# Sums over 64 columns as pairs and fours of array columns, and a row tile's norm moved on VectorE, in a four-layer attention and MLP kernel

## The chip, the cores and the metric

The kernel runs on one core of a Trainium2 chip. The metric is the device time of one execution in microseconds, the median of three runs: 762.07 us before the change (761.74 to 762.75). A core has TensorE (called PE in the profile, with PEld for its weight loads), VectorE (DVE), ScalarE (ACT), GpSimd (POOL), and SyncE (SP), on whose queue this kernel issues its transfers.

## The reference

Four layers follow each other on a sequence of 2048 rows of 576 numbers: attention, MLP, attention, MLP, each behind a layer norm and with a residual. Both attention layers use the same weights, as do both MLP layers. Cut to what matters:

```python
def _A_ref(x, wqkv, wo):
    B, S, D = x.shape
    H = 32; Dh = D // H
    qkv = (x @ wqkv).reshape(B, S, 3, H, Dh).transpose(2, 0, 3, 1, 4)
    q, k, v = qkv[0], qkv[1], qkv[2]
    phi = lambda t: jnp.where(t > 0, t + 1, jnp.exp(t)) + 1e-6
    pq, pk = phi(q), phi(k)
    kv = jnp.einsum("bhsd,bhse->bhde", pk, v)
    z = jnp.einsum("bhsd->bhd", pk)
    num = jnp.einsum("bhqd,bhde->bhqe", pq, kv)
    den = jnp.einsum("bhqd,bhd->bhq", pq, z)[..., None] + 1e-6
    o = num / den
    return o.transpose(0, 2, 1, 3).reshape(B, S, D) @ wo

def _B_ref(x, w1, b1, w2, b2):
    y = _layernorm(x, axis=-1)
    h = _gelu(jnp.einsum("bsd,df->bsf", y, w1) + b1)
    return jnp.einsum("bsf,fd->bsd", h, w2) + b2

for _ in range(2):
    x = x + _A_ref(_layernorm(x, axis=-1), A_wqkv, A_wo)
    x = x + _B_ref(_layernorm(x, axis=-1), B_w1, B_b1, B_w2, B_b2)
```

The attention has no softmax: the sums `kv` and `z` over all rows are made first, and then every query row is multiplied by them.

## The kernel before

**Tiles.** The 2048 rows are 16 row tiles of 128 (`NT`). The 576 columns are four chunks of 128 and a last one of 64. Column halves of 288 (`HALF`) fit one PSUM bank. `yT` holds the normalized rows turned, for the products that contract over columns; `row_of` holds them as they are. The last 64 columns of each row tile lie in `v_ring`, 65 columns to a row tile: 64 of them are data and the 65th is ones (`tail_of(t)` in the second attention layer, which is layer 3 of the four, and `first_tail(t)` in the first).

**An attention layer.** `kv` is not made from `v`. Instead the layer makes K2 = rows-transposed times phi(keys), a matrix of 576 by 576, and multiplies it by the value weights afterwards (`kv_groups`). The column of ones beside the last 64 columns gives `z`, the sum of phi(keys), as row 65 of the last chunk. K2 is made in two column halves, since the accumulators of one half fill the PSUM banks that are to be had:

- *First pass*, one row tile after the other: `k_half(t, 0)` and `k_half(t, 1)` make both halves of the keys (L645), phi is taken on ScalarE and VectorE, one piece of the queries follows (`q_proj`, L614), and `rows_by_keys(t, 0)` adds the row tile to the first half of K2: one matmul for the last 64 columns and the ones (chunk 4, into `k2_tail`, 65 rows) and four for the others.
- *Second pass*: all 16 row tiles' chunk 4 first (L865 and L866: sixteen matmuls of 128 rows by 65 array columns, 288 moving columns), then the four other chunks, two row tiles' worth at a time (`sums`), with other work set between them. `z_stage` (L723 to L731) turns the row of sums into a column, by five matmuls with one column of the identity, and spreads it over the heads on VectorE (`zsel`). `den_stage` (L736) makes the denominators, forty matmuls of 32 array columns and 128 moving ones, whose outputs lie on four groups of 32 PSUM partitions. After them come the logarithm and exponential on ScalarE that make the reciprocal, the spreading of it, `kv_groups`, `kv_wo_half` and the output rows (`wo_stage`).

**Evacuations around the change.** The first half's `k2_tail` goes to `k2[4]`, rows 0 to 64, by one ScalarE copy (L673), ahead of the copies of the other chunks (L686). The second half's goes by one more. `k2[4]` has 128 rows; rows 64 to 127 are zeroed by GpSimd at the layer's start (L635). The value weights' last chunk in `wqkv_sb` likewise has 64 real rows and 64 zeroed ones (L217).

**Row tiles between layers.** While an MLP layer ends, each finished row tile is normalized for the next attention layer in steps (`LNPipe.tick`): statistics (L392, L393), the power -0.5 on GpSimd (L428), the norm into one of three tiles `y_ring` (L465), a store of the rows, and a turn of 32 by 32 blocks on VectorE (L297). Four turned row tiles are stored to DRAM together (L305) and loaded into `yT` (L320, L323). The last row tile (15) is finished when the attention layer has begun, so its statistics are ordered behind a phi on VectorE (`after="phi"`, L1088), while its norm and turn have no such order. `y_ring` is free during the second pass; in the first attention layer its tiles hold some early exponentials (`exp_tile`).

**Order.** TensorE's order is that of the program text (`pe`, L165). The other engines' orders come from a scheduler that keeps data dependencies and manual ones without a signal (`NOSYNC`). SP issues transfers in the order of its queue; at the start they are chained (`chained`, L157), the `x` rows and the attention weights ahead of the MLP weights.

**PSUM.** `ps_h` has four banks with one tag. A matmul into a bank waits for the engine that reads the bank's last content; two more tiles of two banks (`accA`, `accB`) hold the other chunks' sums.

Of the kernel before, what the change touches and what calls it, by code (L numbers as in the profile page):

```python
# [7 lines left out]
ACT = mybir.ActivationFunctionType  # L8
# [26 lines left out]
def build(tc, A_x, A_wqkv, A_wo, B_w1, B_b1, B_w2, B_b2, out, dbg=None, n_layers=4):  # L35
    nc = tc.nc
    dbg = dbg or {}
    with ExitStack() as ctx:
# [167 lines left out]
        for t in range(6, NT):  # L206
            load_x0(t)
        load_wqkv(2)
        nc.vector.memset(y_ring[NY - 1][:], 0.0)
        warm_ps = ps_h.tile([P, 512], F32, name="warm_ps", tag="h")  # L210

# [2 lines left out]
                pe(nc.tensor.matmul(warm_ps[:], lhsT=y_ring[NY - 1][:, 0:P], rhs=y_ring[NY - 1][:, 0:512],  # L214
                                    start=True, stop=True))

        nc.vector.memset(wqkv_sb[64:P, 4, :], 0.0)  # L217
        for vr in v_ring:
            nc.gpsimd.memset(vr[:], 0.0)
            nc.gpsimd.memset(vr[:].rearrange("p g c -> p (g c)")[:, 0:520].rearrange("p (t e) -> p t e", e=65)[:, :, 64:65], 1.0)  # L220
# [73 lines left out]
        def turn_rows(y, t, kind):  # L294

            c, j = divmod(t, TPC)
            turn = nc.vector.transpose(out=turned[:, :, j, :], in_=y[:, 0:D])  # L297
            if dve_last["sum"] is not None:
                tc.add_manual_dep(turn.ins, dve_last["sum"], NOSYNC, reason="rows are turned behind the sums")
            if j < TPC - 1:  # L300
                return
            home = y_d[state["turns"] % 2]
            state["turns"] += 1
            for i in range(4):
                store = nc.sync.dma_start(out=home[:, :, i * P:(i + 1) * P].rearrange("j r n -> r j n"),  # L305
                                          in_=turned[32 * i:32 * (i + 1), :, :, :].rearrange("r j t c -> r j (t c)"))
            landing.append([3, home, c, kind])
            if kind == "A" and c == NCB - 1:
                sp_last["turned"] = store.ins.name
# [32 lines left out]
        class LNPipe:  # L342
# [11 lines left out]
            def tick(self, transposes=1):  # L354
                land()
                for it in list(self.items):
# [77 lines left out]
                    elif st in (2, 3) and it["kind"] == "A" and it["evac"] == "act":  # L434
                        xt, t = it["xt"], it["t"]
                        tail = first_tail(t)[:, 0:64]
                        if it["norm"] == "pool":
                            for out, cols in ((xt[:, 0:4 * P], slice(0, 4 * P)), (tail, slice(4 * P, D))):
                                norm = nc.gpsimd.tensor_scalar(out=out, in0=xt[:, cols], scalar1=it["rstd"][:, 0:1],
                                                               scalar2=it["nmr"][:, 0:1], op0=ALU.mult, op1=ALU.add)  # L440
                            pool_last["norm"] = norm.ins.name
                        else:
                            for name, out, cols in ((f"n{t}", xt[:, 0:4 * P], slice(0, 4 * P)), (f"nt{t}", tail, slice(4 * P, D))):
                                norm = named(name, nc.vector.tensor_scalar(
                                    out=out, in0=xt[:, cols], scalar1=it["mv"][:, 0:1], scalar2=it["rstd"][:, 0:1],
                                    op0=ALU.subtract, op1=ALU.mult))
                            dve_last["norm"] = norm.ins.name
                        row_of[t] = xt
                        it["stage"] = 4
                        continue  # L450
                    elif st in (2, 3):
                        if sum(other["stage"] == 4 for other in self.items) == NY:
                            continue
                        y = y_ring[state["ycnt"] % NY]
                        state["ycnt"] += 1
                        xt = it["xt"]
                        if it["norm"] == "act":
                            nc.scalar.activation(out=y[:, 0:D], in_=xt[:, 0:D], func=ACT.Identity,
                                                 scale=it["rstd"][:, 0:1], bias=it["nmr"][:, 0:1])
                        elif it["norm"] == "pool":  # L460
                            norm = nc.gpsimd.tensor_scalar(out=y[:, 0:D], in0=xt[:, 0:D], scalar1=it["rstd"][:, 0:1],
                                                           scalar2=it["nmr"][:, 0:1], op0=ALU.mult, op1=ALU.add)
                            pool_last["norm"] = norm.ins.name
                        else:
                            norm = nc.vector.tensor_scalar(out=y[:, 0:D], in0=xt[:, 0:D], scalar1=it["mv"][:, 0:1],  # L465
                                                           scalar2=it["rstd"][:, 0:1], op0=ALU.subtract, op1=ALU.mult)
                            dve_last["norm"] = norm.ins.name
                        if it["kind"] == "B" and it["evac"] != "dma":
                            nc.gpsimd.tensor_copy(out=y[:, D:DPAD], in_=y[:, 4 * P:D])
                        if it["kind"] == "A" and it["evac"] == "dma":  # L470
                            c, j = divmod(it["t"], TPC)
                            nc.sync.dma_start(out=yrow_d[c, :, j], in_=y[:, 0:D])
                        it["y"] = y
                        it["stage"] = 4
                        continue
                    elif st == 4:
                        t = it["t"]
                        first_layer = it["kind"] == "A" and it["evac"] == "act"
                        y = it["xt"] if first_layer else it["y"]
                        if it["evac"] == "dma":  # L480
                            turn_rows(y, t, it["kind"])
                            self.items.remove(it)
                            continue
                        tp = ps_h.tile([P, 512], F32, name="tp", tag="h")
                        tp = tp[:, 0:DPAD // 2].bitcast(BF16).rearrange("p (k n) -> p k n", k=KD)
                        first = first_layer and t < 2
                        tp2 = tp
                        if first:
                            tp2 = ps_h.tile([P, 512], F32, name="tp2", tag="h")
                            tp2 = tp2[:, 0:DPAD // 2].bitcast(BF16).rearrange("p (k n) -> p k n", k=KD)  # L490
                        for k in range(KD):
                            block = first_tail(t, P) if first_layer and k == 4 else y[:, k * P:(k + 1) * P]
                            pe(nc.tensor.transpose(out=(tp if k < 3 else tp2)[:, k, :], in_=block, identity=ident[:]))  # L493
                        if first:
                            named(f"ca{t}", nc.scalar.copy(out=yT[:, 0:3, t * P:(t + 1) * P], in_=tp[:, 0:3, :]))
                            named(f"cd{t}", nc.vector.tensor_copy(out=yT[:, 3:KD, t * P:(t + 1) * P], in_=tp2[:, 3:KD, :]))
                        elif it["evac"] == "act":
                            turned_tile = nc.scalar.copy(out=yT[:, :, t * P:(t + 1) * P], in_=tp)
                            act_last["turned"] = turned_tile.ins.name
                            if first_layer and t < 5:  # L500
                                named(f"ca{t}", turned_tile)
                            elif act_last["exp"] is not None:
                                tc.add_manual_dep(turned_tile.ins, act_last["exp"], NOSYNC, reason="keys go on first")
                        else:
                            nc.vector.tensor_copy(out=yT[:, :, t * P:(t + 1) * P], in_=tp)
                        self.items.remove(it)
                        continue
# [100 lines left out]
        def layer_A(li, next_kind, pre_a1=None):  # L608
# [23 lines left out]
            kvwo = {}  # L632
            self_k = dict(pk={}, acc=None, rows={})
            k2 = [blk.tile([P, D], BF16, name="k2", tag="blk") for _ in range(KD)]
            nc.gpsimd.memset(k2[4][64:P, :], 0.0)  # L635
            first_pq = None
            if li == 0:
                first_pq = blk.tile([P, D], BF16, name="pq", tag="blk")
# [21 lines left out]
            def rows_by_keys(t, half, chunks=(4, 0, 1, 2, 3), done=True):  # L660
# [9 lines left out]
                    pe(nc.tensor.matmul(dst, lhsT=lhsT, rhs=pk, start=(t == 0), stop=(t == NT - 1)))  # L670
                cols = slice(half * HALF, (half + 1) * HALF)
                if 4 in chunks and t == NT - 1:
                    nc.scalar.copy(out=k2[4][0:65, cols], in_=self_k["tail"][0:65, 0:HALF])  # L673
                if not done:
                    return
                if t % 2:
# [7 lines left out]
                for i, copy in enumerate((nc.scalar.copy, nc.vector.tensor_copy)):  # L684
                    for j in range(2):
                        copy(out=k2[2 * i + j][:, cols], in_=self_k["acc"][i][:, j, 0:HALF])  # L686

            def kv_groups(groups):

# [33 lines left out]
            def z_stage():  # L723
                zp = ps_h.tile([P, 512], F32, name="z_ps", tag="h")
                for g in range(G):
                    pe(nc.tensor.matmul(zp[0:GR[g], g:g + 1], lhsT=k2[4][:, GO[g]:GO[g] + GR[g]], rhs=ident[:, 64:65],
                                        start=True, stop=True))
                nc.vector.tensor_tensor(out=zsel[0:126, 0:4, :], in0=head_sel[0:126, 0:4, :],
                                        in1=zp[0:126, 0:4].unsqueeze(2).to_broadcast([126, 4, H]), op=ALU.mult)
# [132 lines left out]
                rows_by_keys(NT - 1, 0)  # L862


            for t in range(NT):  # L865
                rows_by_keys(t, 1, (4,), done=False)  # L866
            left = list(range(NT))

            def sums(n):
# [316 lines left out]
```

## Time and profile before

| what | value |
|---|---|
| median of three runs | 762.07 us (761.74 to 762.75) |
| the profiled execution's own time | 762.17 us |
| its span in the trace | 760.5 us |
| instructions in the trace | 15743 |
| TensorE clock granted in the span | 1.0 |
| first attention layer's second-pass tail begins | 59.27 us |
| second attention layer's first key matmul begins | 383.93 us |
| second attention layer's second-pass tail begins | 431.54 us |

The span is counted from the first to the last instruction; the execution's time has 1.7 us more around it. In the timelines a row gives the start, the time from the first start to the last end, the engine, the line, the operation, and output and inputs, with "xN" where N alike follow each other. In brackets stands how long the engine was idle before and what ended that. A matmul's end is modelled and matmuls overlap: where they follow each other, the distance of their starts tells what one costs, not its length.

### The profile page before, as it was taken

Reading aid. Unit: us, or ns where it says so; the run is one execution under the profiler, and the core shown is the slowest. Engines: PE = TensorE matmul, PEld = TensorE weight load, DVE = VectorE, ACT = ScalarE, POOL = GpSimd, SP = SyncE. Lnnn points to the kernel's source line nnn. Section 1 sums busy time; section 2 is a strip of 40 time slices with the busy share of each in tenths; the row PEclk is TensorE's granted clock in tenths of the full one; section 3 lists DMA queues with packets and bytes.
Section 4 is the critical chain, followed back from the end, with each engine's and each line's share of the span. In section 5 each row is a group of like instructions: output and inputs, shape, how many; then the busy total and the mean of one; then the engine's idle time right before and its main releaser. Section 6 shows DMA issues by size and latency. Waiting matters only on the chain.

```text
span 760.5 us, 15743 instructions
## 1 busy us (share of the span) xinstructions
PE 753.6 (99%) x6563; PEld 489.4 (64%) x6563; DVE 270.5 (36%) x685; ACT 327.9 (43%) x729; POOL 117.4 (15%) x194
## 2 busy tenths in 40 slices
PE   8999999999999999999999999999999999999998
PEld 5777754774477457646777777447645754674476
DVE  8876862136033503401357577600230132000000
ACT  5886656205700650263056566660164036205600
POOL 4840241002000301200100005300020020001000
PEclk9999999999999999999999999999999999999999
DMA  8994573026312711320304047530240033011000
GB/s 235 266 320 62 169 269 82 17 64 190 82 40 83 179 51 48 112 65 28 120 24 118 18 137 248 191 83 16 79 115 15 16 125 83 9 32 56 1 10 22
DMA packets 80897, 73.82 MB, mean 97 GB/s; under 512 B 36730, under 2 KB 65466, under 8 KB 80826
## 3 DMA queue, kind: packets, MB, share of 16 engines
q1 hardware_dynamic: 80826, 72.82, 32.9%
q8 instruction: 51, 0.84, 0.4%
q14 instruction: 20, 0.16, 0.1%
HBM read 48.03 MB, written 24.77 MB: 96 GB/s over the span
## 4 chain that ended last, share of the span: by engine, by line
PE 95%; DVE 1%; POOL 1%; ACT 1%; DMA 1%; SPq 0%; issue 0%; POOLq 0%; DVEq 0%
PE m_ps L1077 36%; PE h_ps L1019 20%; PE hp_ps L1019 16%; PE q_ps L614 6%; PE k_ps L645 4%; PE wo_ps L907 4%; PE k_ps L670 4%; PE m_half L1077 1%; PE k_tail L670 1%; PE tp L493 1%; DMA x<-in_A_x_dram 1%; PE kv_ps L695 0%; ACT turned L788 0%; PE rden_ps L784 0%; PE den_ps L743 0%
## 5 line engine op out<-in xcount | busy, mean ns | idle before, releaser
L1077 PE MATMUL m_ps<-w_sb,hT 128*128 128x288 bf16 x2232 | 274.8, 286 | 0.0
L1077 PEld LDWEIGHTS <-hT 128*128 128x128 bf16 x2304 | 224.8, 98 | 59.8 <-issue 3.4
L1019 PEld LDWEIGHTS <-w_sb 64*128 64x128 bf16 x2304 | 124.5, 94 | 136.5 <-issue 1.9
L1019 PE MATMUL hp_ps<-yT,w_sb 64*128 64x512 bf16 x1152 | 178.0, 376 | 0.0
L1019 PE MATMUL h_ps<-yT,w_sb 64*128 64x512 bf16 x1152 | 147.9, 376 | 0.0
L1024 ACT COPY relay_sb<-relay_sb 128x1 f32<-128x1 f32 x144 | 28.7, 199 | 259.8 <-PE h_ps L1019 217.5
L1015 ACT ACTIVATE hT<-h_ps,b1T 128x512 bf16<-128x512 f32 x144 | 91.2, 685 | 44.3 <-PE h_ps L1019 44.3
L428 POOL TENSOR_TENSOR ln_rstd<-ln_u,neg_half 128x1 f32<-128x1 f32 x61 | 35.0, 576 | 444.5 <-DVE ln_u L410 219.5
L1015 ACT ACTIVATE hT<-hp_ps,b1T 128x512 bf16<-128x512 f32 x144 | 91.3, 693 | 0.0
L598 DVE TENSOR_TENSOR xbf<-m_ps,xo 128x576 bf16<-128x576 f32 x15 | 11.4, 758 | 213.6 <-PE m_ps L1077 213.6
L598 DVE TENSOR_TENSOR xo<-m_ps,xo 128x576 f32<-128x576 f32 x16 | 12.1, 758 | 174.9 <-PE m_ps L1077 174.9
L581 POOL TENSOR_TENSOR xo<-xo,b_bc 128x576 f32<-128x576 f32 x32 | 41.1, 1288 | 100.8 <-DMA xo<-x_d 62.9
L1019 PE MATMUL h_ps<-yT,w_tail 64*128 64x512 bf16 x144 | 54.1, 376 | 0.0
L1019 PE MATMUL hp_ps<-yT,w_tail 64*128 64x512 bf16 x144 | 54.1, 376 | 0.0
L614 PE MATMUL q_ps<-yT,wqkv_sb 128*126 128x512 bf16 (+1 forms) x200 | 49.3, 379 | 0.1
L645 PE MATMUL k_ps<-wqkv_sb,yT 128*128 128x288 bf16 x320 | 44.8, 286 | 0.9 <-DVE pk L534 0.8
L907 PE MATMUL wo_ps<-kvwo,pq 126*128 126x288 bf16 (+1 forms) x320 | 43.3, 286 | 0.2
L1019 PEld LDWEIGHTS <-w_tail 64*128 64x128 bf16 x288 | 27.1, 94 | 17.1
L645 PEld LDWEIGHTS <-yT 128*128 128x128 bf16 x320 | 31.0, 98 | 9.7 <-issue 1.0
L907 PEld LDWEIGHTS <-pq 126*128 126x128 bf16 (+1 forms) x320 | 30.3, 97 | 8.8 <-issue 0.6
L614 PEld LDWEIGHTS <-wqkv_sb 128*126 128x126 bf16 (+1 forms) x200 | 25.7, 131 | 11.7 <-issue 0.5
L547 ACT ACTIVATE phi_e<-q_ps 126x512 bf16<-126x512 f32 (+1 forms) x40 | 24.0, 599 | 18.4 <-PE q_ps L614 16.7
(131 smaller groups left out, 592.3 us busy)
## 6 DMA issues: line engine op xcount, KB each, us to landing
xo<-x_d SPq DMA_DIRECT2D x48, 288.0 KB, 3.6
x_d<-xo SPq DMA_DIRECT2D x32, 288.0 KB, 2.6
xl<-x_d SPq DMA_DIRECT2D x24, 288.0 KB, 4.3
y_d<-turned SPq DMA_DIRECT2D x40, 144.0 KB, 3.4
w_sb<-in_B_w_dram SPq DMA_DIRECT2D x6, 864.0 KB, 11.0
yT<-y_d SPq DMA_DIRECT2D x10, 512.0 KB, 4.4
w_sb<-in_B_w_dram SPq DMA_DIRECT2D x9, 512.0 KB, 7.7
x_d<-xn SPq DMA_DIRECT2D x16, 288.0 KB, 3.5
```

The lines of the kernel that those rows point to most:

```text
L428: nc.gpsimd.tensor_tensor(out=rstd[:], in0=it["u"][:], in1=neg_half[:], op=ALU.pow)
L547: exp = nc.scalar.activation(out=e_out, in_=ps_ap, func=ACT.Exp)
L581: nc.gpsimd.tensor_tensor(out=xo[:], in0=xo[:], in1=b2_bc[:], op=ALU.add)
L598: total = nc.vector.tensor_tensor(out=xn[:, cols].rearrange("p (h n) -> p h n", h=2), in0=halves, in1=xo[:, cols].rearrange("p (h n) -> p ...
L614: pe(nc.tensor.matmul(qp[0:GR[g], :], lhsT=wqkv_sb[:, k, GO[g]:GO[g] + GR[g]], rhs=yT[:, k, c * CA:(c + 1) * CA], start=(k == 0), stop=(k ...
L645: pe(nc.tensor.matmul(kp[:, 0:HALF], lhsT=yT[:, k, t * P:(t + 1) * P], rhs=wqkv_sb[:, k, D + half * HALF: D + (half + 1) * HALF], start=(k ...
L670: pe(nc.tensor.matmul(dst, lhsT=lhsT, rhs=pk, start=(t == 0), stop=(t == NT - 1)))
L907: pe(nc.tensor.matmul(wp[:, half, 0:HALF], lhsT=pq[(g, c)][0:GR[g], j * P:(j + 1) * P], rhs=kvwo[g][0:GR[g], half * HALF:(half + 1) * HALF ...
L1015: act_last["gelu"] = nc.scalar.activation(out=to, in_=ps, func=ACT.Gelu_apprx_tanh, bias=b1T[:, f:f + 1], scale=1.0).ins.name
L1019: mm = pe(nc.tensor.matmul(dst[n], lhsT=wt, rhs=mv, start=(seen[n] == 0), stop=(seen[n] == 8)))
L1024: relay = nc.scalar.copy(out=relay_sb[:, 1:2], in_=relay_sb[:, 0:1])
L1077: pe(nc.tensor.matmul(acc[half][:, 0:HALF], lhsT=hT[f][:, j * P:(j + 1) * P], rhs=w2_sb[:, f, half * HALF:(half + 1) * HALF], start=(f == ...
```

## The change

The change has three parts.

1. *The last row tile.* For row tile 15 of an attention layer that follows an MLP, the norm and the turn are each ordered behind the phi that is the latest on VectorE when the program reaches them.
2. *The second pass's last chunk.* `last_rows_by_keys` makes the 65 rows in two tiles instead of one. The row of ones: 32 equal array columns of ones, row tile t on the group of 32 PSUM partitions t mod 4, so that each group holds the sum over four row tiles, 32 times. The 64 columns: row tile t on partitions 0 to 63 or 64 to 127 by t mod 2. The first tile is copied whole to `zk`, scaled by 1/32, and `z_stage` adds its 128 rows with a column of ones. The second is copied whole to `k2[4]`, whose lower 64 rows now meet a second copy of the value weights' last 64 rows in `kv_groups`, which adds the two sums.
3. *What this needs.* `zk` lies in `y_ring[0]`; its first half is zeroed by GpSimd and gets the first pass's row of sums by a ScalarE copy of one row. One more load fills rows 64 to 127 of the value weights' last chunk; the memset at the start leaves them out.

```diff
         load_wqkv(2)
+        chained(nc.sync.dma_start(out=wqkv_sb[64:P, 4, 2 * D:3 * D], in_=A_wqkv[4 * P:D, 2 * D:3 * D]))
...
-        nc.vector.memset(wqkv_sb[64:P, 4, :], 0.0)
+        nc.vector.memset(wqkv_sb[64:P, 4, 0:2 * D], 0.0)
...
             turn = nc.vector.transpose(out=turned[:, :, j, :], in_=y[:, 0:D])
+            if kind == "A" and t == NT - 1:
+                tc.add_manual_dep(turn.ins, dve_last["phi"], NOSYNC, reason="keys go on first")
...
+                            if it["after"] == "phi":
+                                tc.add_manual_dep(norm.ins, dve_last["phi"], NOSYNC, reason="keys go on first")
                             dve_last["norm"] = norm.ins.name
...
-            nc.gpsimd.memset(k2[4][64:P, :], 0.0)
+            nc.gpsimd.memset(k2[4][64:P, 0:HALF], 0.0)
+            zk = y_ring[0][:, 0:D]
...
                 if 4 in chunks and t == NT - 1:
-                    nc.scalar.copy(out=k2[4][0:65, cols], in_=self_k["tail"][0:65, 0:HALF])
+                    nc.gpsimd.memset(zk[:, cols], 0.0)
+                    nc.scalar.copy(out=k2[4][0:64, cols], in_=self_k["tail"][0:64, 0:HALF])
+                    nc.scalar.copy(out=zk[64:65, cols], in_=self_k["tail"][64:65, 0:HALF])
...
+            def last_rows_by_keys():
+                parts = [ps_h.tile([P, 512], F32, name=name, tag="h") for name in ("z_rows", "k2_tail")]
+                for size, part in zip((32, 64), parts):
+                    n = P // size
+                    for t in range(NT):
+                        tail = tail_of(t) if li > 0 else first_tail(t)
+                        lhsT = tail[:, 64:65].to_broadcast([P, 32]) if size == 32 else tail[:, 0:64]
+                        pk = self_k["pk"][(1, t // 2)][:, (t % 2) * HALF:(t % 2 + 1) * HALF]
+                        pe(nc.tensor.matmul(part[size * (t % n):size * (t % n + 1), 0:HALF], lhsT=lhsT, rhs=pk,
+                                            start=(t < n), stop=(t >= NT - n)))
+                nc.scalar.activation(out=zk[:, HALF:D], in_=parts[0][:, 0:HALF], func=ACT.Identity, scale=1.0 / 32)
+                nc.scalar.copy(out=k2[4][:, HALF:D], in_=parts[1][:, 0:HALF])
...
-                    pe(nc.tensor.matmul(zp[0:GR[g], g:g + 1], lhsT=k2[4][:, GO[g]:GO[g] + GR[g]], rhs=ident[:, 64:65],
+                    pe(nc.tensor.matmul(zp[0:GR[g], g:g + 1], lhsT=zk[:, GO[g]:GO[g] + GR[g]],
+                                        rhs=(tail_of(0) if li > 0 else first_tail(0))[:, 64:65],
                                         start=True, stop=True))
...
-            for t in range(NT):
-                rows_by_keys(t, 1, (4,), done=False)
+            last_rows_by_keys()
```

In the instruction order of VectorE that results, the norm of row tile 15 stands nine instructions later, behind the query phi of row tile 5 of the second attention layer, and the turn behind that of row tile 6; before, they stood within row tile 4's key and query phi. TensorE has 32 more matmuls, ScalarE four more instructions, GpSimd two more, and SP one transfer more; the orders are otherwise as before.

## The prediction

> **What bounds the kernel now.** I read the page first, then who waited for whom, then the timeline around the places that the change touches.
>
> ```profile
> span 760.5 us, 15743 instructions
> PE 753.6 (99%) x6563; PEld 489.4 (64%) x6563; DVE 270.5 (36%) x685; ACT 327.9 (43%) x729; POOL 117.4 (15%) x194
> ...
> PE 95%; DVE 1%; POOL 1%; ACT 1%; DMA 1%; SPq 0%; issue 0%; POOLq 0%; DVEq 0%
> ```
>
> TensorE is busy for 99% of the span and holds 95% of the chain that ended last. So only two things count: TensorE work that goes, and TensorE stalls that come or go. Its own waits are four:
>
> ```profile
> PE warm_ps L214 <- DVE y_ring L209: 1.3, 1, 1.3
> PE k_ps L645 <- DVE pk L534: 0.8, 1, 0.8
> PE tp L493 <- DVE x L444: 0.4, 1, 0.4
> PE tp L493 <- POOL y_ring L469: 0.4, 1, 0.4
> ```
>
> The second is in the second attention layer, where VectorE turns the last row tile (start us, length, engine, line):
>
> ```profile
> 397.37 0.23 DVE L532 TENSOR_SCALAR phi_e<-phi_e 128x288 bf16<-128x288 bf16 x1
> 398.19 0.86 DVE L465 TENSOR_SCALAR y_ring<-xo,ln_mv,ln_rstd 128x576 bf16<-128x576 f32 x1 [0.59 <-POOL ln_rstd L428]
> 398.97 0.44 DVE L534 SCALAR_TENSOR_TENSOR pk<-k_ps,phi_e 128x288 bf16<-128x288 f32 x1
> ...
> 397.90 0.78 PE L645 MATMUL k_ps<-wqkv_sb,yT 128*128 128x288 bf16 x5
> 399.46 0.77 PE L645 MATMUL k_ps<-wqkv_sb,yT 128*128 128x288 bf16 x5 [0.79 <-DVE pk L534]
> ```
>
> VectorE waits 0.59 us for the row tile's rstd, normalizes (L465), and only then frees the PSUM bank of the keys (L534), for which TensorE stands still. The second pass's tail, also there:
>
> ```profile
> 431.54 2.12 PE L670 MATMUL k_tail<-pk,v_ring 128*65 128x288 bf16 x16
> 433.50 1.14 PE L670 MATMUL k_ps<-pk,yrow_pair 128*128 128x288 bf16 x8
> ...
> 434.72 1.14 PE L670 MATMUL k_ps<-pk,yrow_pair 128*128 128x288 bf16 x8
> 435.79 0.75 PE L743 MATMUL den_ps<-pq,zsel 127*32 127x128 bf16 x40
> 436.47 1.15 PE L670 MATMUL k_ps<-pk,yrow_pair 128*128 128x288 bf16 x8
> ```
>
> Starts count here, since matmuls overlap: sixteen tail matmuls take 433.50 - 431.54 = 1.96 us, 0.1225 each. The denominators' forty matmuls of 32 columns take 0.68.
>
> **Part 1, the last row tile's norm and turn.** A row tile of the key loop takes 2.915 us of TensorE (401.76, 404.68, 407.60: starts of k_ps). The one with the stall takes 401.76 - 397.90 = 3.86. The stall is worth **0.945 us**. In the new VectorE order the norm stands behind the pq of row tile 5, the turn behind that of row tile 6. Without the norm, L534 follows L532 at 397.60 and ends at 398.06, before TensorE wants the bank at 397.90 + 0.61 = 398.51.
>
> What is late next: from a row tile's start s, the steady order is L534 at s+2.14, the last pq at s+3.62 to 4.05, the next key step at s+4.17 (row tile starting 404.68: 406.82, 408.30, 408.85). The norm enters at s+4.02, takes 0.86, and pushes the next row tile's L534 from 2.14 to about 2.73, end 3.19. The bank is wanted at 2.915 + 0.61 = 3.525: 0.33 to spare, so I charge nothing; without that cover the price is up to the stall removed, 0.945. The turn (0.77) is shorter and fits likewise.
>
> The turn moves from 399.58 to about 404.85. Behind it on SP's queue stand the row store L472, four stores L305, the yT loads L320 and L323, the tail load L328, four row loads L290 and the xo loads L574, all some 5.25 us later. L320 is issued at 405.88 now, L323 at 406.31; then at 411.1 and 411.6. The longest landing of any L323 is 5.3 us, so 416.9. Row tile 12, the first reader, starts at 419.26 now, 418.3 then: 1.4 us of cover. The tail and rows are read only after 421, xo from 453.
>
> **Part 2, the tails.** Out: 1.96 us in each attention layer. In: sixteen matmuls of 32 columns in fours, sixteen of 64 columns in pairs. The nearest row for fours is den_ps: ten fours in 0.68 us. One 128-column matmul alone takes 0.055 (four transposes, 32.57 to 32.79), so a four costs about what one costs; the rest is the change of shape: 0.09 into it (435.79 - 434.72 - 8 x 0.1225), 0.10 out. So 4 x 0.1225 + 8 x 0.1225 = 1.47, plus 0.09, plus 0.10, plus the change from 32 to 64 columns. For that no row exists; 0 if it is free, 0.19 if it is an exit and an entry; I take 0.09, one change. New tail 1.75, gain **0.21** a layer (0.11 to 0.30). Pairs of 64 columns have no row either: from perfect sharing (0.98) to none (1.96); I take sharing, nearest to den_ps, which differs only in width.
>
> The Trainium skill, TensorEngine Tiling (Array Packing), Key Properties, says that a change of tiling mode drains TensorE. The trace agrees for den_ps (0.09 and 0.10); by that rule 32 to 64 is such a change too, so the sum stays; without it the gain would be 0.30 a layer.
>
> ScalarE gets one more evacuation in each half (the one row of sums; in the second, z_rows): 0.28 us of pace (57.67 to 57.95). In the second attention layer it is hidden: L686 ends at 432.48, then 432.8, wanted at about 433.3. In the first, the delay runs through pq and the mask casts into zsel, 62.75 becoming 63.03; its 0.28 and a 0.06 signal end at 63.37, while den_ps could start at 63.30. It costs **0.05** there. The sums for z are evacuated while the 64-column pairs run and are ready 0.6 us before z_stage. The z matmuls keep shape and number.
>
> **Part 3, small edits.** GpSimd's two memsets of 128x288 (about 0.3 us: 128x640 takes 0.63): in layer 1 behind row tile 5 at 18.7, before an rstd that starts at 18.97, under 0.1 late, with transposes 1.5 us later. In the second attention layer it waits for the turn at 384.80 to 385.57, with the pq memset (0.52) behind it: done at 386.5, first needed at 387.61. The load of 64 wqkv rows, 0.52 us of SP issue at 15.4, delays the w1, w2, wo, bias and first xo loads; no wait of TensorE names these weights, and it stands behind the x loads. The start-up memset shrinks by a third of 0.78, but the next statistics (3.03) follow x, issued at 0.79 and landing 2.2 later. All nothing.
>
> **Sum.** 0.945 + 0.21 + 0.21 - 0.05 = 1.3 us. The profiled execution took 762.17 (span 760.5 and 1.7 around it), 0.1 above the median of 762.07: 760.87 by it, **760.8** against the median, 0.17% faster.
>
> **Rivals.**
> - *The shape change costs nothing, or runs are kinder.* With 32 to 64 free, 0.18 more goes: 760.6. Against: each change of shape in the trace costs 0.09 to 0.10. Run scatter (1.0 us over three) can then carry the measured time past 0.2%.
> - *The stall moves instead of going.* Norm or turn at the new place holds a key bank: for it, 0.33 us of cover is thin and ScalarE's pace sets phi; against, VectorE idles 0.9 us in each row tile (0.54, 0.19, 0.2). Price up to 0.945: 761.7.
> - *The columns do not share the array* (the slower one). Place: the two tails. If all 32 matmuls run one by one, a tail takes 32 x 0.1225 + 0.19 = 4.1, 2.15 more; two are 4.3, less 0.945: +3.35, 765.4. If only pairs fail, 0.98 a layer more than forecast: 762.7. The kernel is slower once a tail exceeds 2.43 us (0.945 / 2 above 1.96), by over 0.2% once it exceeds 3.2. Against: den_ps shares; in the trace its fours start 0.056 apart. For: its operands are 128 wide, not 288, and no row has 64 columns.
> - *The weight loads do not hide.* If in the new shapes a load stands ahead of its matmuls, 0.095 a four (as den_ps's loads last) and 0.11 a pair (as the tail's) give 4 x 0.095 + 8 x 0.11 = 1.26 a layer: 763.3. Against: den_ps's loads of 0.095 run within steps of 0.056. The Trainium skill, TensorEngine Tiling (Array Packing), Gotcha 2, says that column tiling excludes fast weight load; no run here shows what that does to 64 columns.
> - *Turned rows come too late.* Past 1.4 us of cover TensorE waits one for one at row tile 12; a load 2 us slower than any seen gives 761.4. Against: the longest landing was used.
>
>
> **How the numbers follow.** Forecast 0.62 (760.8, own range 760.3 to 761.3), kinder case 0.12, moved stall 0.11, no sharing in whole or part 0.08, loads not hidden 0.02, late rows 0.05. 0.2% is 1.5 us, about what a measurement of this kernel can tell from no change: faster means below 760.55. The forecast lies 0.25 above that; scatter of some 0.3 puts a third of it beyond, with most of the kinder case: faster 0.32. Slower, above 763.6: the whole loss of sharing (0.05) and late rows or a moved stall dearer than their bounds (0.03): 0.08. Within: 0.60. The range 760.1 to 762.6 takes in the moved stall and most of the late rows.
>
> **What would show it.** Right: k_ps no longer waits for L534 near 398; every key row tile takes 2.915 us; from the first z_rows to the next k_ps start about 1.75 us, fours 0.12 apart, pairs 0.12 apart. Wrong: a k_ps or q_ps wait for VectorE near 403 to 407, a wait for DMA at row tile 12, pairs 0.24 apart, or den_ps in layer 1 later than sums plus 0.1.

## The result and the profile after

The changed kernel takes 760.45 us (median of 13 runs, 760.37 to 761.17); the kernel before, run beside it, 762.05 (13 runs, 761.45 to 762.81). The ratio is 0.9982, with a 95% interval of 0.9975 to 0.9989: 1.6 us, or 0.18%, faster. The forecast was 760.8 and 0.17%. The profiled execution of the changed kernel took 760.39 us.

From the page of the changed kernel, the lines that answer to the first two shown of before:

```profile
span 758.7 us, 15815 instructions
...
PE 752.8 (99%) x6595; PEld 487.6 (64%) x6595; DVE 271.6 (36%) x685; ACT 328.8 (43%) x733; POOL 116.6 (15%) x196
```

TensorE has 32 matmuls more and is busy for 0.8 us less. The span is 1.8 us shorter, so about one us of it was TensorE standing still. Its waits in the changed kernel (total, times, longest; two of the start-up, of 1.3 and 0.2 us, are left out):

```profile
...
PE k_ps L652 <- ACT yT L501: 0.3, 1, 0.3
...
PE den_ps L767 <- DVE zsel L752: 0.2, 1, 0.2
```

The wait of k_ps for the key step of VectorE is gone. That of k_ps for yT stands at 6.47 us, in the start-up, and a second trace of the kernel before has it too. The one that is new with the change is den_ps's: it waits for zsel, in the first attention layer. VectorE in the second attention layer, after (start, length):

```profile
397.01 0.23 DVE L538 TENSOR_SCALAR phi_e<-phi_e 128x288 bf16<-128x288 bf16 x1
397.27 0.46 DVE L540 SCALAR_TENSOR_TENSOR pk<-k_ps,phi_e 128x288 bf16<-128x288 f32 x1
...
401.56 0.57 DVE L469 TENSOR_SCALAR y_ring<-xo,ln_mv,ln_rstd 128x576 bf16<-128x576 f32 x1
...
402.87 0.46 DVE L540 SCALAR_TENSOR_TENSOR pk<-k_ps,phi_e 128x288 bf16<-128x288 f32 x1
...
404.68 0.77 DVE L299 STREAM_TRANSPOSE turned<-y_ring 128x576 bf16<-128x576 bf16 x1
```

L540 (L534 of before) now stands right behind L538, and the norm (L469) comes four us later, with the turn (L299) another three behind. TensorE there:

```profile
397.54 1.39 PE L652 MATMUL k_ps<-wqkv_sb,yT 128*128 128x288 bf16 x10
...
400.45 1.39 PE L652 MATMUL k_ps<-wqkv_sb,yT 128*128 128x288 bf16 x10
```

All ten key matmuls of row tile 5 run in one piece, and row tiles follow each other at 2.915 us. The tail of the second attention layer:

```profile
430.32 0.67 PE L706 MATMUL z_rows<-pk,v_ring 128*32 128x288 bf16 x16
430.93 1.17 PE L706 MATMUL k_tail<-pk,v_ring 128*64 128x288 bf16 x16
432.03 1.15 PE L677 MATMUL k_ps<-pk,yrow_pair 128*128 128x288 bf16 x8
```

The tail takes 432.03 - 430.32 = 1.71 us from its first start, against 1.96.

Where the span of the two traces differs, stage by stage (us; a stage runs from the start of one matmul to the start of another). The last column is a second trace of the kernel before, taken among the experiments:

| stage | before | after | before, second trace |
|---|---|---|---|
| start to the last matmul ahead of the first tail | 59.05 | 58.60 | 58.58 |
| that matmul to the end of the tail, layer 1 | 2.18 | 2.02 | 2.18 |
| tail to den_ps, layer 1 | 2.29 | 2.54 | 2.29 |
| den_ps of layer 1 to the first key matmul of layer 3 | 320.42 | 320.41 | 320.41 |
| first key matmul to the last matmul ahead of the tail, layer 3 | 47.49 | 46.54 | 47.95 |
| that matmul to the end of the tail, layer 3 | 2.08 | 1.92 | 2.08 |
| tail to den_ps, den_ps to the output rows, layer 3 | 17.20 | 17.20 | 17.19 |
| output rows to the last MLP | 24.66 | 24.41 | 24.60 |
| last MLP to the end | 285.11 | 285.05 | 285.11 |

The change made 0.95 (keys of layer 3) + 0.16 + 0.16 (tails) - 0.25 (den_ps in layer 1) = 1.02 us of this. Another 0.70 comes and goes without it: 0.45 of start-up, which the second trace of before is shorter by as well, and 0.25 behind the output rows of layer 3, where two traces of the changed kernel show 24.41 and 24.66. The last 0.06 lies behind the issue of the last store. It does go with the change: every trace of a kernel with the new tails has 285.04 or 285.05 in the last row, every other one 285.11 or 285.12. What causes it stays open. The second trace of before also shows the stall in the keys larger than the first one does: 47.95 - 46.54 = 1.41 us instead of 0.95.

### The profile page after: what moved, and what is told of

Its sections match the earlier page's. It is cut to its first block, busy times and chain, and to the rows that moved or that the text cites. A ratio compares the mean times of both kernels' runs of the same rounds, so it can differ in the third digit from the quotient of the medians.

```text
span 758.7 us, 15815 instructions
## 1 busy us (share of the span) xinstructions
PE 752.8 (99%) x6595; PEld 487.6 (64%) x6595; DVE 271.6 (36%) x685; ACT 328.8 (43%) x733; POOL 116.6 (15%) x196
## 4 chain that ended last, share of the span: by engine, by line
PE 96%; DVE 2%; ACT 1%; issue 0%; DMA 0%; DVEq 0%
PE m_ps L1100 36%; PE h_ps L1042 21%; PE hp_ps L1042 16%; PE q_ps L620 6%; PE k_ps L652 5%; PE wo_ps L930 4%; PE k_ps L677 4%; PE m_half L1100 1%; PE tp L499 1%; PE k_tail L677 1%; PE kv_ps L718 0%; PE den_ps L767 0%; PE rden_ps L808 0%; DVE xo L604 0%; PE kvwo_half L736 0%
```

## The experiments

**The norm and the turn alone**, on the kernel before:

```diff
+            if kind == "A" and t == NT - 1:
+                tc.add_manual_dep(turn.ins, dve_last["phi"], NOSYNC, reason="keys go on first")
...
+                            if it["after"] == "phi":
+                                tc.add_manual_dep(norm.ins, dve_last["phi"], NOSYNC, reason="keys go on first")
```

> The kernel before with only the two orders on VectorE: norm and turn of row tile 15 behind the phi. My theory (the parts add, each acting on TensorE alone): the stall of 0.945 us at row tile 5 of the second attention layer goes, no new one comes; 0.95 us faster, ratio 0.9988; in the trace every key row tile takes 2.915 us and nothing else moves but what follows earlier. Rival (the gain of 1.6 us comes mostly from elsewhere, the start or the output rows of layer 3): ratio nearer 0.9995, or the norm alone gives 1.2 us and more because the output rows profit too.

**The tails and small edits alone**: the changed kernel without these four lines.

> The changed kernel without the two orders: tails as fours and pairs, extra evacuations, memsets and load. My theory: each tail gives 0.16 us of TensorE; the first attention layer gives it back, since den_ps waits 0.24 us for zsel behind ScalarE's extra copy; so 0.1 us faster in sum, ratio 0.9999, and the stall of 0.945 stays. Rival (the start-up profits from the shorter memset, by the 0.44 us that the two profiles differ there): ratio 0.9993 and the first steady key row tile 0.44 us earlier in the trace.

With the first, 760.87 us (ratio to before 0.9986, interval 0.9977 to 0.9995); with the second, 761.66 (0.9996, 0.9987 to 1.0005). On the same chip the kernel before took 761.95 (761.73 to 762.8) and the changed kernel again 760.73 (0.9985, 0.9976 to 0.9994):

> The changed kernel once more, beside its parts on the same chip. Theory: 1.6 us faster as before, of it 0.95 the norm; if the parts add, its ratio is the product of those of the two parts alone. In the trace, what is mechanism repeats (key row tiles of 2.915, tails of 1.71, den_ps wait of 0.17), and what is chance differs: the start-up (0.44 earlier in the first trace) and the wait for GpSimd's y_ring copy in the output rows (0.25).

By the medians, then, the order on VectorE is worth 1.08 us, the rest 0.29 with an interval that holds zero, and both together 1.22. The traces say it more exactly: with the order alone the keys of layer 3 take 46.54 and the tails 1.96; with the tails alone 47.49 and 1.71. Of the waits of TensorE with the order alone, one has no like in the traces before and after:

```profile
...
PE wo_ps L911 <- DVE xn L602: 0.3, 1, 0.3
```

No key matmul waits for pk. The line shown is a wait in the output rows of layer 1. With it that stage took 24.33 us instead of 23.77, and this execution 761.43, 0.56 above the kernel's median. It came in one more run below; what causes it stays open.

**The row of sums by VectorE.** The theory for the new den_ps wait: in layer 1 ScalarE evacuates the first half's 64 rows of sums and the row of ones by two copies instead of one, and everything behind them is late. One line gives the second copy to VectorE:

```diff
-                    nc.scalar.copy(out=zk[64:65, cols], in_=self_k["tail"][64:65, 0:HALF])
+                    nc.vector.tensor_copy(out=zk[64:65, cols], in_=self_k["tail"][64:65, 0:HALF])
```

> The changed kernel, the copy of the first half's one row of sums moved from ScalarE to VectorE. My theory: ScalarE's two copies cost 0.41 us of pace each where one cost 0.28, and the 0.5 us so lost reach zsel in the first attention layer; without it den_ps waits no more, 0.24 us faster than the changed kernel, nothing in the second attention layer. Rival (zsel is late because of VectorE's own casts, not ScalarE): den_ps waits as long or longer, since VectorE has one more copy; no gain or up to 0.2 us lost.

ScalarE in the first attention layer of the kernel before, one copy of 65 rows with the next copy behind it:

```profile
57.67 0.39 ACT L673 CAST k<-k_tail 65x288 bf16<-65x288 f32 x1
57.95 0.71 ACT L686 CAST k<-k_ps 128x288 bf16<-128x288 f32 x2
```

The changed kernel's timeline there:

```profile
57.21 0.39 ACT L681 CAST k<-k_tail 64x288 bf16<-64x288 f32 x1
...
57.62 0.39 ACT L682 CAST y_ring<-k_tail 1x288 bf16<-1x288 f32 x1
...
58.04 0.70 ACT L695 CAST k<-k_ps 128x288 bf16<-128x288 f32 x2
...
62.82 0.28 DVE L752 TENSOR_TENSOR zsel<-head_sel,z_ps 126x128 bf16<-126x128 bf16 x1
...
63.15 0.75 PE L767 MATMUL den_ps<-pq,zsel 127*32 127x128 bf16 x40 [0.17 <-DVE zsel L752]
```

And with the row on VectorE:

```profile
57.46 0.39 ACT L681 CAST k<-k_tail 64x288 bf16<-64x288 f32 x1
...
57.73 0.70 ACT L695 CAST k<-k_ps 128x288 bf16<-128x288 f32 x2
58.06 0.46 DVE L682 CAST y_ring<-k_tail 1x288 bf16<-1x288 f32 x1
...
63.15 0.75 PE L767 MATMUL den_ps<-pq,zsel 127*32 127x128 bf16 x40
```

ScalarE goes from the 64 rows to the next copy in 57.73 - 57.46 = 0.27 us, as from the 65 rows before (57.95 - 57.67 = 0.28); with the row between them it took 58.04 - 57.21 = 0.83. Without it den_ps waits for nothing: 2.30 us from the end of the tail to den_ps instead of 2.54. The time is 760.49 (0.9981, 0.9973 to 0.9990), 0.24 below the changed kernel on the same chip, as the trace says, though the two intervals overlap. The theory holds by the trace, and this version has the lowest time of those that ran there.

**The memset of the start-up**: the kernel before with a third of VectorE's zeroing given to GpSimd.

```diff
-        nc.vector.memset(wqkv_sb[64:P, 4, :], 0.0)
+        nc.vector.memset(wqkv_sb[64:P, 4, 0:2 * D], 0.0)
+        nc.gpsimd.memset(wqkv_sb[64:P, 4, 2 * D:3 * D], 0.0)
```

> The kernel before, VectorE's memset at the start cut to the same 64x576 words as in the changed kernel; GpSimd zeroes the rest. My theory: the first statistics follow the landing of x, not the memset, so nothing is gained, ratio 1.0000, and the 0.4 us by which the first attention layer's keys run earlier in the changed kernel's traces are scatter of the first loads. Rival (the shorter memset starts the chain earlier): 0.3 to 0.4 us faster, ratio 0.9996, with the first pass's last query matmuls 0.4 us earlier than in the trace of before.

761.67 us, 1.0001 of the kernel before (0.9992 to 1.001), whose median on that chip was 761.79. The unchanged kernel again:

> The kernel before, for one more profile. Theory: the stall of 0.945 us at row tile 5 of the second attention layer and both tails of 1.96 us repeat; the moment of the first attention layer's last query matmul (59.05 in the first trace) scatters by some tenths of a us with the first loads. Rival: 59.05 repeats within 0.1, and the 0.4 us less of the changed kernel are its own.

One execution, 762.13. Its start-up (58.58) is as short as that of the changed kernel (58.60) and of this one (58.68): the 0.45 us between the first two traces is not the memset.

**The same columns one after the other.** The theory that it is text order that makes matmuls share: four (or eight) row tiles in a row go to one group of columns, then to the next.

```diff
-                        pe(nc.tensor.matmul(part[size * (t % n):size * (t % n + 1), 0:HALF], lhsT=lhsT, rhs=pk,
-                                            start=(t < n), stop=(t >= NT - n)))
+                        place, each = t * n // NT, NT // n
+                        pe(nc.tensor.matmul(part[size * place:size * (place + 1), 0:HALF], lhsT=lhsT, rhs=pk,
+                                            start=(t % each == 0), stop=(t % each == each - 1)))
```

> The changed kernel with the same 32 matmuls in each tail, but matmuls that follow each other on the same array columns (row tiles 0 to 3 on the first group of 32 and so on). Theory (fours and pairs share the array): nothing overlaps now, each matmul takes 0.1225, sixteen of 32 columns 1.96 where fours took 0.60, sixteen of 64 columns 1.96 where pairs took 1.10; 2.2 us a layer, 4.4 us in sum, 762.9 to 763.6 measured, slower than before by some 0.4%, less what den_ps's wait of 0.17 us hides. Rival (the pairs of array columns are not what makes the tail short): less than 1 us.

761.34 us (0.9994, 0.9985 to 1.0003): most of the expected loss did not come. TensorE in layer 3:

```profile
430.69 0.70 PE L707 MATMUL z_rows<-pk,v_ring 128*32 128x288 bf16 x16
431.33 1.69 PE L707 MATMUL k_tail<-pk,v_ring 128*64 128x288 bf16 x16
432.95 1.15 PE L677 MATMUL k_ps<-pk,yrow_pair 128*128 128x288 bf16 x8
```

The fours take 431.33 - 430.69 = 0.64, as before (0.61). The pairs take 1.62 instead of 1.10: by single starts (the start of each matmul by itself, which the merged rows leave out) five matmuls run alone 0.12 us apart, then the second half's chain begins 0.006 after the fifth of them and the two run side by side. So the groups need not alternate in the text for matmuls to share: with four in a row on a group nearly all of the sharing stayed, with eight in a row on a half part of it was lost. Where between four and eight it begins to be lost, and whether the width matters, was not run.

**Nearly all on one group.** To price the case without sharing, thirteen of the sixteen 32-column matmuls go to one group and fifteen of the sixteen 64-column ones to one half:

```diff
-                        pe(nc.tensor.matmul(part[size * (t % n):size * (t % n + 1), 0:HALF], lhsT=lhsT, rhs=pk,
-                                            start=(t < n), stop=(t >= NT - n)))
+                        place = t if t < n else 0
+                        pe(nc.tensor.matmul(part[size * place:size * (place + 1), 0:HALF], lhsT=lhsT, rhs=pk,
+                                            start=(t < n), stop=(t == NT - 1 or 0 < t < n)))
```

> The changed kernel, but of the sixteen matmuls of 32 columns thirteen go to one group of array columns (each of the others gets one), and of the sixteen of 64 columns fifteen go to one half. Theory (what is shared is the columns: matmuls overlap when they are on different groups, in whatever order they stand, and those on one group follow each other at 0.1225 us): thirteen steps, then fifteen; the start of z_rows to the next k_ps 12 x 0.1225 + 0.225 + 14 x 0.1225 + 0.25 = 3.66 us instead of 1.71, 1.95 more in each attention layer, of which the first layer's wait for zsel (0.24) takes a little; the time 3.5 to 3.9 us above the changed kernel, about 764.2. Rival (narrow matmuls are cheap by themselves, whatever group they are on): a tail of 1.7 to 2.3 us and a time within 1.2 us of the changed kernel.

```profile
432.09 1.77 PE L707 MATMUL z_rows<-pk,v_ring 128*32 128x288 bf16 x16
433.78 2.03 PE L707 MATMUL k_tail<-pk,v_ring 128*64 128x288 bf16 x16
435.74 0.54 PE L677 MATMUL k_ps<-pk,yrow_pair 128*128 128x288 bf16 x3
```

435.74 - 432.09 = 3.65 (3.66 expected), and 764.10 us, 1.0026 of before (1.0016 to 1.0037), whose median here was 762.04. What the tails gain is the sharing by groups of columns, nothing else about narrow matmuls.

**The turn left free**: the changed kernel, but only the norm is ordered.

```diff
-            if kind == "A" and t == NT - 1:
-                tc.add_manual_dep(turn.ins, dve_last["phi"], NOSYNC, reason="keys go on first")
```

> The changed kernel with the norm ordered behind the phi, the turn left free: the scheduler then puts the turn one instruction behind the norm, in the same row tile. Theory (there is 0.33 us of cover beside a norm of 0.59 to 0.86): norm and turn together push the freeing of the key bank past TensorE's need by 0.3 to 0.5 us; a k_ps waits there again, and the kernel is 0.3 to 0.5 us slower than the changed one. Rival (VectorE's idle 0.9 us a row tile swallows both): no wait, same time as the changed kernel.

760.51 us (0.9983, 0.9974 to 0.9992), and no wait of k_ps:

```profile
401.79 0.58 DVE L467 TENSOR_SCALAR y_ring<-xo,ln_mv,ln_rstd 128x576 bf16<-128x576 f32 x1
...
402.42 0.77 DVE L299 STREAM_TRANSPOSE turned<-y_ring 128x576 bf16<-128x576 bf16 x1
...
403.56 0.46 DVE L538 SCALAR_TENSOR_TENSOR pk<-k_ps,phi_e 128x288 bf16<-128x288 f32 x1
403.60 1.39 PE L650 MATMUL k_ps<-wqkv_sb,yT 128*128 128x288 bf16 x10
```

Norm and turn stand in one row tile, and L538 still ends at 404.02, before TensorE wants the bank at 403.60 + 0.61 = 404.21. VectorE goes from the norm to L538 without a pause, so with a norm of 0.86 us, which I had taken from the trace of before, L538 would have ended about 0.28 later, at 404.30, just too late (an estimate).

**The norm without GpSimd's memsets.** Why is the same norm 0.86 long in one place and 0.57 in another? In the second trace of before it lasts 1.32:

```profile
397.72 1.32 DVE L465 TENSOR_SCALAR y_ring<-xo,ln_mv,ln_rstd 128x576 bf16<-128x576 f32 x1 [0.59 <-POOL ln_rstd L428]
```

There, as in the first trace, GpSimd has just made ln_rstd and goes on to three memsets of ones into query tiles; the view of GpSimd in the first trace of before:

```profile
398.21 1.91 POOL L622 MEMSET pq<- 32x512 bf16 x3
```

In single starts the norm of the first trace (398.19) ends 0.37 after the second memset begins, and that of the second trace 0.37 after the third begins. So it looks as if the norm stood behind one memset in the first and two in the second. (Of the four traces in which the norm keeps its old place and the memsets their own, three show 0.86 and one 1.32.) The first trace had more to say of it. Row tile 14's norm, in the MLP layer ahead, has a single memset beside it and is 0.86 us long again:

```profile
378.62 0.86 DVE L465 TENSOR_SCALAR y_ring<-xo,ln_mv,ln_rstd 128x576 bf16<-128x576 f32 x1 [0.73 <-POOL ln_rstd L428]
378.64 0.52 POOL L622 MEMSET pq<- 32x512 bf16 x1
```

Of the trace's forty norms of this shape, the 23 beside which GpSimd does nothing take 0.56 to 0.58 us, and ten that start 0.07 us behind the start of a GpSimd addition of 1.28 us take 1.52. The Trainium skill, SBUF — State Buffer, in the section SBUF: two separate sides, says that VectorE and GpSimd share one pair of ports under an exclusive lock, held for a whole instruction, and that tensor_scalar can be an instruction that takes it. To test it, the three memsets of the kernel before wait for the norm:

```diff
+                            if it["after"] == "phi":
+                                pool_last["row"] = norm.ins.name
+                                tc.add_manual_dep(pool_last["ones"].ins, norm.ins.name, SYNC, reason="the norm goes first")
...
-                        (nc.gpsimd if li > 0 else nc.vector).memset(pq[(g, c)][96:P, 0:CA], 1.0)
+                        ones = (nc.gpsimd if li > 0 else nc.vector).memset(pq[(g, c)][96:P, 0:CA], 1.0)
+                        pool_last["ones"] = ones
+                        if li > 0 and "row" in pool_last:
+                            tc.add_manual_dep(ones.ins, pool_last["row"], SYNC, reason="the norm goes first")
```

> The kernel before, with the norm of the last row tile where it was; only GpSimd's three memsets of ones into the query tiles, which began 0.02 us after that norm in the traces of before, now wait for it. Theory (the norm is held up by those memsets: 0.86 us and 1.32 us in two traces of before beside them, 0.57 us in the trace of the changed kernel where they are past): the norm takes 0.57, the key step behind it starts about 0.48 after the norm instead of 0.78 to 1.24, and the stall of the key matmul is about 0.65 us whether the attention layer starts early or late; from the layer's first key matmul to the second pass's tail 47.1 to 47.25 us (47.49 and 47.95 before, 46.54 without a stall). The time is 0.3 to 0.75 us under before. Rival (a norm behind a wait simply takes 0.86 or more, the memsets beside it do nothing): the norm stays at 0.86 or longer, the stall at 0.95 to 1.4, the time that of before within 0.2.

```profile
398.42 0.58 DVE L465 TENSOR_SCALAR y_ring<-xo,ln_mv,ln_rstd 128x576 bf16<-128x576 f32 x1 [0.59 <-POOL ln_rstd L428]
398.91 0.45 DVE L537 SCALAR_TENSOR_TENSOR pk<-k_ps,phi_e 128x288 bf16<-128x288 f32 x1
```

```profile
399.14 1.69 POOL L625 MEMSET pq<- 32x512 bf16 x3 [0.76 <-DVE y_ring L465]
```

The norm takes 0.58 us, L537 follows 0.49 behind its start, and the keys of layer 3 take 47.21, as expected: the stall is 0.67. The time is 761.36, 0.68 below before on that chip (0.9992, 0.9983 to 1.0001). The interval reaches just past 1, so the reading rests on the traces. (This execution had the wait in layer 1's output rows again, 0.5 us; its own time was 761.88.) So of the stall of before about 0.67 us is the norm standing ahead of the key step and waiting for ln_rstd, and 0.28 or 0.74 more is the norm held up by one or two memsets. That the lock is what holds it up agrees with the rule, but the runs show only that it happens beside the memsets and not without them. By the recorded starts the norm comes first, by 0.02 us (398.19 and 398.21), and is the one that waits all the same; the runs do not show why.

## Why the prediction was right, and where its terms were off

The time (760.45 for 760.8) and the sign were right. Step by step:

- **The norm's order, 0.945: the mechanism and this trace's size right, too small in some executions.** L540 starts at 397.27, behind L538 at 397.01, as worked out, and the keys gain 0.95 us. But the stall that goes was 1.41 us in one of the four traces that have the old order with the memsets beside it. The step treated the norm's 0.86 as its own length; 0.29 of it was the memset beside it, as the quiet norms of the same trace could have told. The order alone measured 1.08.
- **The cover behind the new place, 0.33 us to spare: right that it holds, wrong in size by about the same 0.29.** L540 of row tile 6 starts 402.87 - 400.45 = 2.42 after its row tile, not 2.73, and leaves 3.525 - 2.42 - 0.46 = 0.65. It was wide enough for the turn as well, as the run with the turn left free shows, so the turn's new place carries nothing.
- **The turn's later transfers: nothing, right.** The turn started at 404.68 (404.85 forecast), the yT loads were issued at 410.59 and 411.02 (411.1, 411.6), and row tile 12 started at 417.95 (418.3) with no wait for a transfer. The forecasts count in the trace of before, where this layer starts 0.36 us later (383.93, not 383.57), so row tile 12 came as forecast and the turn some 0.2 later.
- **The tails, 0.21 a layer: the mechanism right, the size 0.16.** The forecast tail of 1.75 counts the entry, which lies ahead of its first start; measured so, it is 1.71 + 0.094 = 1.80. By single starts the entry cost 0.094 and the exit 0.10, as taken, and most steps between are 0.12. From the last four to the first pair it is 0.225, 0.10 above a step, so "I take 0.09" for the change of shape that had no row was near. What the sum lacked is that the first step behind a change of shape is slower as well: 0.133 between the first fours and 0.147 between the first pairs, 0.01 and 0.025 above 0.1225. That is most of the 0.05 by which the tail was longer than forecast. The Trainium skill, TensorEngine Tiling (Array Packing), Key Properties, says that changing the tiling mode drains TensorE; the trace agrees, now for 32 to 64 columns too, with 0.10.
- **ScalarE's extra copy in layer 1, 0.05: far too small, 0.25.** The step that failed is "0.28 us of pace (57.67 to 57.95)". That was the pace from the 65-row copy to the next; the copy of a single row between them cost 0.83 - 0.27 = 0.56. zsel started 62.82 - 58.91 = 3.91 us after the tail's first start, where the forecast had 63.03 - 59.27 = 3.76. Of the forecast's own signs of being wrong this one came: den_ps in layer 1 later than the sums by more than 0.1. With 0.25 lost of 0.32 won, parts 2 and 3 were worth 0.07 us by these stages, 0.13 with the 0.06 at the end.
- **Part 3, nothing: right.** The shorter memset gained nothing on its own, and GpSimd's memsets in layer 3 ended at 386.19 (forecast 386.5, again counted in the trace of before).
- **The rivals.** A tail with hardly any sharing takes 3.65 us, as the run with nearly all on one group shows; the forecast had 4.1 for none at all. The weight loads stayed hidden: fours and pairs run at the pace of a single matmul, 0.12 us.

So the mechanisms were right, and that their sum of 1.3 us lies so near is in part luck, since its terms were off in both directions: a stall of 0.945 where executions show 0.95 to 1.41, tails 0.42 where they gave 0.32, 0.05 where 0.25 was lost, and nothing for the 0.06 at the end. By these the change is worth 1.08 to 1.54. Measured were 1.22 beside the experiments and 1.6 at first, whose interval goes from 0.8 to 1.9; nothing in it asks for a further cause.

## What to carry to other kernels

The length of an instruction in a trace is not its price elsewhere: look at what the neighbouring engine did at the same moment before it goes into a sum, and take it from rows where that engine is quiet (here 23 of forty, in the same trace). A wait at the head of an in-order engine costs through what is queued behind it, so moving the waiting instruction behind the one that frees a buffer gains the whole stall, and then the gap it moves into matters only by its width. When one matmul becomes two kinds that share the array, count what evacuates the second result: a copy of one row on ScalarE cost TensorE 0.25 us here, more than the tail gained in that layer.

## What the runs showed that was not expected

- Matmuls of different column groups overlap although they do not alternate in the text. With four in a row on each group, sixteen ran as four steps; with eight in a row on each half, the second chain began 0.006 us after the fifth start of the first.
- A norm of 128x576 (float32 to bfloat16) on VectorE takes 0.56 to 0.58 us alone, 0.86 when it stands behind one memset of GpSimd, 1.32 behind two, and 1.52 when an addition of 1.28 us has begun on GpSimd 0.07 us before it. For row tile 15 it ended 0.37 us after the second memset had begun, or after the third.
- Two ScalarE copies that read one PSUM tile, 64 rows and then one, start 0.41 us apart, and the copy behind them again 0.42; without the second, 0.27. Why a single row takes that long was not settled.
